# Re-ordering the first tiles of a retention layer with a gated feed-forward: a decay table and v scaled on GpSimd, narrow ups in one bank, half downs with attention steps placed by hand

## The chip, the cores and the metric

The kernel runs on one core of a Trainium2 chip. The metric is the device time of one execution in microseconds; lower is better. Before the change it was 242.91 us (median of 3 runs, 242.81 to 243.11). The span that a profile shows is 1.7 us shorter than the time of the same run. All ratios below are the mean time of one kernel's fast runs over that of the kernel before in the same rounds on the same chip, so they are not quite the ratio of the medians quoted.

## The reference

A retention layer runs token by token for 4 batches and 8 heads of 64, over 768 tokens; its output feeds a feed-forward layer with a sigmoid gate (3072 tokens, 512 wide, 1536 hidden).

```python
def _attn_ref(q, k, v):                       # q, k, v: (4, 8, 768, 64)
    gamma = 1.0 - 2.0 ** (-5.0 - np.arange(H))
    for t in range(S):
        state = gamma * state + outer(k[:, :, t], v[:, :, t])
        y[:, :, t] = scale * (q[:, :, t] @ state)

def _moe_ref(x, w_gate, w_val, w_out):        # x: (3072, 512)
    gate = 1.0 / (1.0 + np.exp(-(x @ w_gate)))
    return (gate * (x @ w_val)) @ w_out
```

## The kernel before

The sequence is cut into 24 chunks of 128 tokens (6 per batch). Within a chunk the recurrence becomes masked matrix products ("scores", "intra"), between chunks a state is carried ("state", "inter"). Decay enters through two tables: `tabv` scales v before use, `taby` scales y on its way out of PSUM. Four chunks make one tile of 512 tokens; a tile needs 12 "ups" (8 matmuls each, gate and value) and 4 "downs" (12 matmuls each). Attention of the next tile is woven between the ups and downs of this one. The order of the program text is the order on every engine: nothing is rescheduled.

Words used below: PE is TensorE, which does the matmuls; in lines of the profile DVE is VectorE, ACT is ScalarE, POOL is GpSimd, and L with a number is a line of that run's kernel. PSUM is the memory that matmuls write, in banks; an eviction copies a result out of it. The granted clock is the share of its full clock that PE was given. Of the tiles, qkT holds the turned q and k of a chunk, sA and sB its scores, vs its scaled v, z its state, y its result and xT that result scaled for the feed-forward; gs is the sigmoid of a gate, hT the product of gate and value, hT(0,0) that of tile 0's first up, and ob a down's result on its way out.

```python
    def load_chunk(g):                # k and q cast to bf16 on the way, v as float32;
        load_kq(g)                    # all issued by GpSimd, as are the weights
        load_v(g, nc.gpsimd)

    def make_taby(cols):              # decay table of y, on ScalarE
        for p in range(NP):
            nc.scalar.activation(taby[:, p, cols], toky[:, cols], AX.Exp, scale=lgp[:, p:p + 1], bias=lsc)

    def transposes(g):                # k, q of a chunk, turned on PE, evicted by ScalarE
        ...
        nc.scalar.activation(qkT[g], tp, AX.Copy)

    def scale_v(g, eng):
        eng.tensor_tensor(vs[g], vf[g], tabv[:, g % NCH, :].unsqueeze(2).to_broadcast([C, H, D]), op=ALU.mult)

    def y_out(g):                     # VectorE
        nc.vector.tensor_tensor(xT[g // 4][:, :, col:col + C], y[g], taby[:, :, c * C:(c + 1) * C], op=ALU.mult)

    def step_t(g):
        if g < XBAR:                  # XBAR = 12: later chunks are transposed by DMA
            transposes(g)
        scale_v(g, nc.vector if g < 8 else nc.gpsimd)

    def step_y(g, nxt=None):
        inter(g)
        if nxt is not None:
            scores(nxt)
        state(g); intra(g); state_out(g)
        if nxt is not None:
            masks(nxt)                # VectorE
        y_out(g)

    def up(t, n1, lo=0, hi=512):      # pf is a ring of three PSUM banks, tag "ff"
        ps = []
        for w in (wg, wv):
            u = pf.tile([128, 512], F32, tag="ff", name="ff")
            ...                       # 4 matmuls
            ps.append(u)
        nc.scalar.activation(gs[:, lo:hi], ps[0][:, lo:hi], AX.Sigmoid)
        nc.vector.tensor_tensor(hT[t][:, n1, lo:hi], gs[:, lo:hi], ps[1][:, lo:hi], op=ALU.mult)

    def keep_on(n):                   # matmuls of no use, meant to keep PE's clock up; they take a bank of the ring too
        u = pf.tile([128, 512], F32, tag="ff", name="ff")
        for _ in range(n):
            nc.tensor.matmul(u[:, :128], ident, ident, start=True, stop=True)

    ...
    scale_v(2, nc.vector)             # the start, chunk after chunk (cut)
    y_out(1)
    ...
    make_taby(slice(512, 768))
    nc.scalar.preload_act_table(AX.Sigmoid)
    intra(2)
    y_out(2)
    scale_v(3, nc.vector)
    keep_on(8)
    up(0, 0, 0, 384)
    transposes(3)
    up(0, 1, 0, 384)
    scores(3)
    ...
    for t in range(NT):
        groups = [lambda n1=n1: up(t, n1) for n1 in range(0 if t else 4, NFF)]
        groups += [lambda sm=sm: down(t, sm) for sm in range(4)]
        steps = attention(t + 1) if t + 1 < NT else []      # nine steps
        ...
        for i, group in enumerate(groups):
            group()
            upto = -(-len(steps) * (i + 1 - first) // (len(groups) - first))
            ...                       # steps spread evenly behind the groups
```

## Time and profile before

| | |
|---|---|
| time | 242.91 us |
| PE busy | 228.8 us (95% of the span) |
| ScalarE, VectorE, GpSimd busy | 95.0, 101.4, 91.5 us |
| PE idle, 0 to 28.65 us | 5.3 us, and 9.0 us of keep-warm matmuls |
| PE idle, 40.7 to 62.2 us | 3.1 us |
| PE idle, 62.2 to 206.1 us | 0.0 us |

The table is read from the bottom: the last row says that the steady tiles have nothing to give, so a gain must come from the first 62 us. A busy PE there is not a useful PE, as the keep-warm matmuls count too. The lines of the profile that carry this stand in the prediction.

### The profile page before, as it was taken

The numbers are of one execution on the slowest core, as the hardware profiler recorded it, in microseconds if no ns is written. First come the engines' busy times: TensorE is split into PE (matmuls) and PEld (weight loads), VectorE is DVE, ScalarE is ACT, GpSimd is POOL, SyncE is SP. The second block draws the span as 40 slices with busy tenths as digits, with TensorE's granted clock in tenths as the row PEclk, the third lists the DMA queues.
The fourth block names the chain that finished last, engine by engine and source line by source line (L and its number), as shares of the span: only waits on it lengthen the run. The fifth ranks groups of instructions, "written<-read, shape, count | busy, mean of one in ns | idle before, by whom it ended". The sixth has DMA issues, their size and how long they took to land.

```text
span 241.1 us, 4300 instructions
## 1 busy us (share of the span) xinstructions
PE 228.8 (95%) x1720; PEld 118.0 (49%) x1720; DVE 101.4 (42%) x168; ACT 95.0 (39%) x179; POOL 91.5 (38%) x111
## 2 busy tenths in 40 slices
PE   7689998998899999999999999999999999999993
PEld 6565644554445554444554445444445554444441
DVE  2565534474256623256632255642256641243300
ACT  7778434343544432334333324232233431333221
POOL 8986674887899446883101101111000000000000
PEclk9999999999999999999999999999999999999999
DMA  8999999999999999999932383002200012100022
GB/s 144 178 200 197 195 208 200 186 196 228 233 179 119 117 153 187 196 160 157 151 51 87 109 91 67 0 16 83 79 3 0 0 46 83 47 3 0 0 87 87
DMA packets 77267, 27.27 MB, mean 113 GB/s; under 512 B 65024, under 2 KB 72704, under 8 KB 77248
## 3 DMA queue, kind: packets, MB, share of 16 engines
q0 software_dynamic: 57616, 16.78, 72.9%
q1 hardware_dynamic: 18592, 9.97, 20.2%
q10 hardware_dynamic: 1040, 0.26, 0.5%
q8 instruction: 13, 0.21, 0.4%
q14 instruction: 6, 0.05, 0.1%
HBM read 28.31 MB, written 6.29 MB: 144 GB/s over the span
## 4 chain that ended last, share of the span: by engine, by line
PE 90%; ACT 7%; issue 1%; DVE 0%; POOL 0%; POOLq 0%; ACTq 0%
PE ff L242 51%; PE ff L252 26%; PE sA L160 3%; ACT qkT L140 3%; PE y L196 2%; ACT taby L123 2%; PE z L182 2%; PE y L172 2%; PE tp L138 2%; PE ff L262 2%; ACT zbd L190 1%; ACT L315 1%; ACT ob L255 0%; ACT gs L246 0%; DVE xT L204 0%
## 5 line engine op out<-in xcount | busy, mean ns | idle before, releaser
L247 DVE TENSOR_TENSOR hT<-gs,ff 128x512 bf16<-128x512 f32 (+2 forms) x76 | 50.0, 659 | 80.3 <-PE ff L242 76.8
L242 PE MATMUL ff<-xT,wg 128*128 128x512 bf16 (+2 forms) x304 | 74.7, 368 | 1.2 <-DVE xT L204 1.1
L242 PE MATMUL ff<-xT,wv 128*128 128x512 bf16 (+2 forms) x304 | 74.6, 368 | 0.0
L246 ACT ACTIVATE gs<-ff 128x512 f32<-128x512 f32 (+2 forms) x76 | 43.7, 574 | 69.3 <-PE ff L242 69.3
L252 PE MATMUL ff<-wo,hT 128*128 128x512 bf16 x288 | 65.0, 379 | 0.0
L242 PEld LDWEIGHTS <-wv 128*128 128x128 bf16 x304 | 29.3, 98 | 33.2
L242 PEld LDWEIGHTS <-wg 128*128 128x128 bf16 x304 | 27.9, 98 | 31.3 <-issue 1.4
L252 PEld LDWEIGHTS <-hT 128*128 128x128 bf16 x288 | 27.3, 98 | 32.1
L150 POOL TENSOR_TENSOR vs<-vf,tabv 128x512 bf16<-128x512 f32 x16 | 16.5, 1046 | 51.2 <-PE y L196 46.3
L255 ACT COPY ob<-ff 128x512 f32<-128x512 f32 x24 | 14.1, 586 | 55.0 <-PE ff L252 50.7
L62 POOL DMA_DIRECT2D vf<-in_v_dram x23 | 20.7, 901 | 12.7 <-DMA kn<-in_k_dram 8.3
L204 DVE TENSOR_TENSOR xT<-y,taby 128x512 bf16<-128x512 f32 x24 | 16.4, 683 | 20.6 <-PE y L196 20.6
L165 DVE TENSOR_TENSOR stA<-sA,causal 128x512 bf16<-128x512 f32 x24 | 16.5, 687 | 19.9 <-PE sB L160 19.9
L67 POOL DMA_DIRECT2D kn<-in_k_dram x23 | 20.8, 905 | 5.7 <-DMA qn<-in_q_dram 1.7
L68 POOL DMA_DIRECT2D qn<-in_q_dram x23 | 20.4, 888 | 3.1 <-DMA wo<-in_moe_w_out_dram 1.7
L190 ACT CAST zbd<-z 64x256 bf16<-64x256 f32 x40 | 14.7, 367 | 12.2 <-PE z L182 11.9
L166 DVE TENSOR_TENSOR stB<-sB,causal 128x512 bf16<-128x512 f32 x24 | 16.3, 680 | 0.0
L140 ACT ACTIVATE qkT<-tp 128x1024 bf16<-128x1024 bf16 x12 | 12.3, 1024 | 4.9 <-PE tp L138 4.8
L262 PE MATMUL ff<-ident 128*128 128x128 bf16 x104 | 9.0, 252 | 1.6 <-POOL ident masks.py:199 1.6
L160 PE MATMUL sA<-qkT 64*128 64x128 bf16 x48 | 4.7, 219 | 5.5 <-ACT qkT L140 5.4
L196 PE MATMUL y<-stA,vs 128*64 128x128 bf16 x96 | 9.9, 222 | 0.0
L196 PE MATMUL y<-stB,vs 128*64 128x128 bf16 x96 | 9.5, 221 | 0.0
(40 smaller groups left out, 107.7 us busy)
## 6 DMA issues: line engine op xcount, KB each, us to landing
out_dram<-ob SPq DMA_DIRECT2D x24, 256.0 KB, 2.0
vf<-in_v_dram POOLq DMA_DIRECT2D x23, 256.0 KB, 8.9
kn<-in_k_dram POOLq DMA_DIRECT2D x23, 128.0 KB, 8.8
qn<-in_q_dram POOLq DMA_DIRECT2D x23, 128.0 KB, 9.1
wg<-in_moe_w_gate_dram POOLq DMA_DIRECT2D x6, 256.0 KB, 8.7
wv<-in_moe_w_val_dram POOLq DMA_DIRECT2D x6, 256.0 KB, 9.1
wo<-in_moe_w_out_dram POOLq DMA_DIRECT2D x4, 384.0 KB, 10.7
qf<-in_q_dram ACTq DMA_DIRECT2D x1, 256.0 KB, 4.5
```

The source lines that it names most:

```text
L62: eng.dma_start(out=vf[g], in_=src(v, g))
L67: nc.gpsimd.dma_start(out=kn[g], in_=src(k, g))
L68: nc.gpsimd.dma_start(out=qn[g], in_=src(q, g))
L140: nc.scalar.activation(qkT[g], tp, AX.Copy)
L150: eng.tensor_tensor(vs[g], vf[g], tabv[:, g % NCH, :].unsqueeze(2).to_broadcast([C, H, D]), op=ALU.mult)
L165: nc.vector.tensor_tensor(stA[g], sc[g][0], causal4, op=ALU.mult)
L190: nc.scalar.copy(zbd[g % 2][half, :, half], zps[b][half])
L196: nc.tensor.matmul(y[g][i * D:(i + 1) * D, p, :], vs[g][:, 2 * p + i, :], st[:, p, :], start=(first and p == 0), stop=True, skip_group_che ...
L242: nc.tensor.matmul(u[:, lo:hi], w[:, kk, n1 * 128:(n1 + 1) * 128], xT[t][:, kk, lo:hi], start=(kk == 0), stop=(kk == KT - 1))
L246: nc.scalar.activation(gs[:, lo:hi], ps[0][:, lo:hi], AX.Sigmoid)
L247: nc.vector.tensor_tensor(hT[t][:, n1, lo:hi], gs[:, lo:hi], ps[1][:, lo:hi], op=ALU.mult)
L252: nc.tensor.matmul(o, hT[t][:, n1, sm * 128:(sm + 1) * 128], wo[:, n1, :], start=(n1 == 0), stop=(n1 == NFF - 1))
```

## The change

Its intent: start the feed-forward earlier and leave no wait in the first tile. On ScalarE, the Exp table is loaded at once and half of `taby` is no longer made there; GpSimd multiplies the first half by a constant per head instead. GpSimd also scales v of chunks 0 and 1. The last 128 columns of the first four ups share a bank each for gate and value. Downs are cut in halves, and the attention steps of tile 0's loop stand at places chosen by hand. At the start of tile 1, the first two ups are split so that chunk 7's last step can come between them. The order of the steps of chunks 0 to 2 and the keep-warm matmuls among them changed too; that part of the diff is cut. The core of the diff:

```diff
-    nc.scalar.dma_start(out=qf, in_=src(q, 0))
+    nc.sync.dma_start(out=qf, in_=src(q, 0))
+    nc.scalar.preload_act_table(AX.Exp)
 ...
+    def extend_taby():
+        nc.gpsimd.tensor_tensor(taby[:, :, 384:768], taby[:, :, 0:384],
+                                gup.unsqueeze(2).to_broadcast([128, NP, 384]), op=ALU.mult)
 ...
+    scale_v(0, nc.gpsimd)
     load_gate_val(0)
+    scale_v(1, nc.gpsimd)
     load_chunk(3)
+    load_gate_val(1)
+    load_gate_val(2)
+    make_taby(slice(0, 256))
 ...
+    make_taby(slice(256, 384))
+    extend_taby()
 ...
-    make_taby(slice(512, 768))
-    nc.scalar.preload_act_table(AX.Sigmoid)
     intra(2)
     y_out(2)
     scale_v(3, nc.vector)
     keep_on(8)
     up(0, 0, 0, 384)
+    up(0, 1, 0, 384)
     transposes(3)
-    up(0, 1, 0, 384)
+    keep_on(16)
     scores(3)
 ...
-    for n1 in range(4):
-        up(0, n1, 384, 512)
+    up_columns(0, range(4), 384, 512)      # four ups' last columns side by side in one bank
 ...
+        groups, steps, place = ups(t) + downs(t), [], []      # downs(t): two halves each
+        if t == 0:
+            groups = groups[4:]
+            steps = [step_t(4), step_s(4), step_y(4), step_t(5), step_s(5),
+                     step_t(6), step_y(5, 6), step_t(7), step_y(6, 7)]      # lambdas left out
+            place = [4, 5, 7, 9, 10, 11, 12, 13, 14]
+        elif t + 1 < NT:
+            steps = attention(t + 1)
+            place = [0, 1, 3, 5, 7, 8, 10, 13, 17]
+        if t == 1:
+            groups[:2] = [up(1, 0, 0, 384), step_y(7), up(1, 1, 0, 384), up_columns(1, range(2), 384, 512)]
+            place = [p + 2 for p in place]
```

More of the change, by code (lines that the diff above doesn't have):

```diff
@@ L97 @@
     make_identity(nc, ident)
-    toky = const.tile([128, S], I32, name="toky")
-    nc.gpsimd.iota(toky, pattern=[[1, S]], base=0, channel_multiplier=0)
+    toky = const.tile([128, 384], I32, name="toky")
+    nc.gpsimd.iota(toky, pattern=[[1, 384]], base=0, channel_multiplier=0)
     load_chunk(1)
@@ L115 @@
         nc.vector.memset(lgp[D:128, p:p + 1], lg[2 * p + 1])
+    gup = const.tile([128, NP], F32, name="gup")
+    for h in range(H):
+        nc.vector.memset(gup[h % 2 * D:(h % 2 + 1) * D, h // 2:h // 2 + 1], math.exp(384 * lg[h]))
     zbd = [const.tile([128, NP, C], BF16, name=f"zbd{i}") for i in range(2)]
@@ L247, in up, with up_columns, down @@
         nc.vector.tensor_tensor(hT[t][:, n1, lo:hi], gs[:, lo:hi], ps[1][:, lo:hi], op=ALU.mult)
-    def down(t, sm):
-        o = pf.tile([128, 512], F32, tag="ff", name="ff")
-        for n1 in range(NFF):
+    def up_columns(t, n1s, lo, hi):
+        n = hi - lo
+        ps = []
+        for w in (wg, wv):
+            u = pf.tile([128, 512], F32, tag="ff", name="ff")
+            for i, n1 in enumerate(n1s):
+                for kk in range(KT):
+                    nc.tensor.matmul(u[:, i * n:(i + 1) * n], w[:, kk, n1 * 128:(n1 + 1) * 128], xT[t][:, kk, lo:hi],
+                                     start=(kk == 0), stop=(kk == KT - 1))
+            ps.append(u[:, :len(n1s) * n])
+        gs = ffn.tile([128, 512], F32, tag="gs", name="gs")
+        g = gs[:, :len(n1s) * n]
+        nc.scalar.activation(g, ps[0], AX.Sigmoid)
+        nc.vector.tensor_tensor(hT[t][:, n1s[0]:n1s[-1] + 1, lo:hi], g.rearrange("p (i n) -> p i n", n=n),
+                                ps[1].rearrange("p (i n) -> p i n", n=n), op=ALU.mult)
+    po = {}
+    def down(t, sm, part):
+        if part == 0:
+            po[0] = pf.tile([128, 512], F32, tag="ff", name="ff")
+        o = po[0]
+        half = NFF // 2
+        for n1 in range(part * half, (part + 1) * half):
             nc.tensor.matmul(o, hT[t][:, n1, sm * 128:(sm + 1) * 128], wo[:, n1, :],
                              start=(n1 == 0), stop=(n1 == NFF - 1))
+        if part == 0:
+            return
         ob = ffn.tile([128, D_MODEL], F32, tag="ob", name="ob")
@@ L262, in keep_on @@
             nc.tensor.matmul(u[:, :128], ident, ident, start=True, stop=True)
+    scale_v(0, nc.gpsimd)
     load_gate_val(0)
+    scale_v(1, nc.gpsimd)
     load_chunk(3)
-    for s in range(1, NFF // 2):
+    load_gate_val(1)
+    load_gate_val(2)
+    make_taby(slice(0, 256))
+    kn[0] = ld.tile([C, H, D], BF16, tag="kn", name="kn")
+    qn[0] = ld.tile([C, H, D], BF16, tag="qn", name="qn")
+    nc.vector.tensor_copy(kn[0], kf)
+    nc.scalar.copy(qn[0], qf)
+    keep_on(36)
+    transposes(0)
+    make_taby(slice(256, 384))
+    extend_taby()
+    for s in range(3, NFF // 2):
         load_gate_val(s)
@@ L273 @@
         load_chunk(g)
-    kn[0] = ld.tile([C, H, D], BF16, tag="kn", name="kn")
-    qn[0] = ld.tile([C, H, D], BF16, tag="qn", name="qn")
-    make_taby(slice(0, 256))
-    nc.vector.tensor_copy(kn[0], kf)
-    nc.scalar.copy(qn[0], qf)
-    keep_on(36)
-    transposes(0)
     keep_on(8)
-    scale_v(0, nc.vector)
     scores(0)
+    masks(0)
+    keep_on(8)
+    transposes(1)
+    inter(0)
     state(0)
     state_out(0)
-    masks(0)
-    keep_on(8)
-    make_taby(slice(256, 384))
-    transposes(1)
-    scale_v(1, nc.vector)
-    inter(0)
     intra(0)
     y_out(0)
-    keep_on(10)
+    keep_on(8)
     scores(1)
+    masks(1)
+    keep_on(4)
+    inter(1)
     state(1)
     state_out(1)
-    masks(1)
-    inter(1)
-    keep_on(10)
-    make_taby(slice(384, 512))
     transposes(2)
+    nc.scalar.preload_act_table(AX.Sigmoid)
     intra(1)
+    y_out(1)
     scale_v(2, nc.vector)
-    y_out(1)
     keep_on(12)
     scores(2)
+    masks(2)
+    inter(2)
     state(2)
     state_out(2)
-    masks(2)
-    inter(2)
-    keep_on(12)
-    make_taby(slice(512, 768))
-    nc.scalar.preload_act_table(AX.Sigmoid)
+    keep_on(10)
     intra(2)
@@ L331, with ups, downs @@
     up(0, 3, 0, 384)
-    for n1 in range(4):
-        up(0, n1, 384, 512)
-    for t in range(NT):
-        groups = [lambda n1=n1: up(t, n1) for n1 in range(0 if t else 4, NFF)]
-        groups += [lambda sm=sm: down(t, sm) for sm in range(4)]
-        steps = attention(t + 1) if t + 1 < NT else []
+    up_columns(0, range(4), 384, 512)
+    def ups(t):
+        return [lambda n1=n1: up(t, n1) for n1 in range(NFF)]
+    def downs(t):
+        return [lambda sm=sm, i=i: down(t, sm, i) for sm in range(4) for i in range(2)]
+    for t in range(NT):
+        groups, steps, place = ups(t) + downs(t), [], []
+        if t == 0:
+            groups = groups[4:]
+            steps = [lambda: step_t(4), lambda: step_s(4), lambda: step_y(4), lambda: step_t(5), lambda: step_s(5),
+                     lambda: step_t(6), lambda: step_y(5, 6), lambda: step_t(7), lambda: step_y(6, 7)]
+            place = [4, 5, 7, 9, 10, 11, 12, 13, 14]
[3 more added lines that the diff above has]
+        if t == 1:
+            groups[:2] = [lambda: up(1, 0, 0, 384), lambda: step_y(7), lambda: up(1, 1, 0, 384),
+                          lambda: up_columns(1, range(2), 384, 512)]
+            place = [p + 2 for p in place]
         if t + 2 < NT:
@@ L342 @@
                 load_chunk(g)
-        first = 0 if t else 6
-        done = 0
         for i, group in enumerate(groups):
-            if i == len(groups) - 5:
+            if i == len(groups) - 9:
                 for g in range(4 * t + 8, 4 * t + 12):
@@ L350 @@
             group()
-            upto = -(-len(steps) * (i + 1 - first) // (len(groups) - first))
-            while done < min(upto, len(steps)):
-                steps[done]()
-                done += 1
+            for p, step in zip(place, steps):
+                if p == i:
+                    step()
 _INS = ['q', 'k', 'v', 'moe_w_gate', 'moe_w_val', 'moe_w_out']
```

## The prediction

> **What bounds the kernel now.** I read the page first, then the chain that ended last, the waits of the PE, the stretches by window, and the timeline of the first 65 us with the landings of its loads.
>
> ```profile
> PE   7689998998899999999999999999999999999993
> ACT  7778434343544432334333324232233431333221
> DMA  8999999999999999999932383002200012100022
> ```
>
> Each digit is 6 us. PE is full from about 28 us to the end, apart from a dip between 40 and 62; in the windows view 62.15 to 206.10 holds 143.95 us of PE in 143.95. So only the first 62 us can give anything. The feed-forward is fixed: a 512-wide up (8 matmuls) takes 1.73 us and a down (12) 2.59 in the chain, so six tiles need 6 x (12 x 1.73 + 4 x 2.59) = 186.7 us whatever the order. DMA is near full from the start: a second possible bound there.
>
> The chain (start, length, what):
>
> ```profile
> 13.26 1.65 ACT taby L123 x4
> 14.93 1.03 ACT qkT L140
> ...
> 17.51 2.07 ACT taby L123 x4
> 19.60 1.28 ACT L315
> 20.89 0.49 ACT gs L246
> 21.39 0.92 ACT qkT L140
> 22.35 0.23 PE sA L160
> ...
> 41.38 1.03 ACT qkT L140
> ...
> 56.03 1.03 ACT qkT L140
> ...
> 61.41 0.70 DVE xT L204
> ```
>
> Until 22 us ScalarE is the bound: the decay tables (taby) stand in its queue ahead of the transposes' evictions (qkT), then the sigmoid table load, and chunk 3's scores start only at 22.35. Later PE waits three times where an attention step follows the work it needs too closely.
>
> ```profile
> PE sA L160 <- ACT qkT L140: 5.4, 5, 1.3
> PE ff L242 <- DVE xT L204: 1.1, 2, 0.8
> ```
>
> Of these the timeline puts 1.12 at 42.46, 1.18 at 57.11 and 0.79 at 62.15: 3.09 us between 40 and 62, which agrees with the windows view (18.34 busy in 21.42). The timeline of the first ups:
>
> ```profile
> 11.59 0.96 POOL L62 DMA_DIRECT2D vf<-in_v_dram  x1
> 15.96 0.75 POOL L81 DMA_DIRECT2D wg<-in_moe_w_gate_dram  x1 [0.43 <-DMA wv<-in_moe_w_val_dram]
> 18.88 0.68 DVE L150 TENSOR_TENSOR vs<-vf,tabv 128x512 bf16<-128x512 f32 x1
> 19.02 0.81 PE L242 MATMUL ff<-xT,wg 128*128 128x384 bf16 x4 [0.30 <-DVE xT L204]
> 26.32 0.39 PE L242 MATMUL ff<-xT,wg 128*128 128x128 bf16 x4
> 28.65 1.02 PE L242 MATMUL ff<-xT,wg 128*128 128x512 bf16 x4
> ```
>
> The first line is the load of chunk 3's v, which the tile view says takes 7.0 us to land: at 18.6, just before VectorE scales it (18.88). First up at 19.02, last columns from 26.32, first full-width up at 28.65. I count from these marks.
>
> **What the Trainium skill says.** (1) "SBUF — State Buffer", Who interferes with whom: a VectorE instruction with two SBUF inputs and a GpSimd instruction that reads SBUF exclude each other for the whole instruction; the later one blocks. scale_v is such an instruction, masks and evictions (one PSUM input) are not. Before, GpSimd computes nothing with it in the first 60 us, so the trace cannot show this. (2) "GPSIMD Engine Reference", Elementwise — side-by-side cycle accounting: about 2.6 cycles an element for two inputs, GpSimd some 2x slower. The trace agrees in kind:
>
> ```profile
> L150 POOL TENSOR_TENSOR vs<-vf,tabv 128x512 bf16<-128x512 f32 x16 | 16.5, 1046 | 51.2 <-PE y L196 46.3 <-issue 4.9
> L150 DVE TENSOR_TENSOR vs<-vf,tabv 128x512 bf16<-128x512 f32 x8 | 5.5, 684 | 1.7 <-DMA vf<-in_v_dram 1.7
> ```
>
> (3) "ScalarE: Activation LUTs", Table-load gate, puts a load at about 2.7 us with its drain; here the row reads 1.28, so I use that. (4) "TensorE: Matmul & The Clock Gate", Back-to-back issue gap and its phases: 55.6 ns a 128-wide matmul, 215.7 a 512-wide. The trace: 0.22 us for four and 1.73 for eight. It agrees.
>
> **The change part by part.**
>
> ScalarE. taby for columns 384 to 767 leaves it: 1.65 + 2.07 = 3.72 us of the chain above; the third 128 columns move ahead of the second qkT. The Exp table load starts about 0.5 earlier. Walking the new order with these durations: qkT0 ends 7.3, taby 9.0, qkT1 10.0, z of chunk 0 after v on GpSimd (about 9.1), zbd0 10.8, scores(1) 10.2, z of chunk 1 waits for GpSimd's second v (11.6), zbd1 12.7, qkT2 13.7, table load 15.0, masks(2) 15.6, y_out(2) 16.7. The first up then starts at about 16.8, 2.3 us earlier.
>
> GpSimd. It is also the issuer of loads. iota loses 0.38 (half of 0.77). Two v scalings add 2 x 1.05. The taby extension, 1536 columns, is an estimate of 3 x 1.05 = 3.1 us. After walking: v0 at 8.0 to 9.05, wg0 issued 9.0 (before 8.38), v1 10.5 to 11.55, chunk 3's v issued at 13.25 (before 11.59), extension from about 17.1 to 20.2, then the fourth weight slab at 20.2 (before 15.96). The delays mostly eat queueing: loads took 5.0 us while the queue was short and 7 to 10 later. I put chunk 3's v at 19.0 (before 18.6). Slab 1 lands about 21.5 and is wanted after 22; later weights keep 2 us or more.
>
> VectorE. In its order chunk 3's scaling stands ahead of the first hT. That was harmless (hT waited for the sigmoid until 21.42); with the first up ending at 18.1 it is a new wait. hT(0,0) comes after the load at 19.0 plus 0.3 plus 0.69, and, if the skill's exclusion holds, only after the extension (20.2). The 16 keep-warm matmuls take the PSUM buffer that hT(0,0) frees (ring of three, counted through the allocations), and scores(3) stand behind them. So scores(3) start at 19.3 + 0.69 + 0.55 + 1.0 = about 21.6 without exclusion, 20.3 + 2.25 = about 22.6 with it; before 22.35. Of the 2.3 us won, -0.2 to 0.8 remain at this place.
>
> Columns. The 32 narrow matmuls took 28.65 - 26.32 = 2.33 with 0.33 of waiting for a bank; in one bank 32 x 0.055 = 1.76. Gain 0.6. First full-width up: 27.3 without, 28.3 with exclusion. Gain 1.35 or 0.35.
>
> Attention between half downs in tile 0. With a step between half downs (1.3 us each) or ups, qkT (1.03) has time. I find small waits left: 0.15 for qkT5 and qkT7 (the ob copy stands ahead of them on ScalarE), 0.35 for y_out(6) before tile 1's first up (masks(7) precede it), 0.25 for qkT8 after the two short columns. 3.09 - 0.75 = 2.3 us gained.
>
> Steady tiles. The hand places 0,1,3,5,7,8,10,13,17 over 20 groups are what the old formula gave over 16, with a down counted as two halves: no change. The tail too: 0.
>
> Sum: 1.35 + 2.3 = 3.65, or 0.35 + 2.3 = 2.65. 242.91 less these is 239.3 or 240.3. As some later waits (a short load, a bank) can also vanish with the narrow ups, I take **239.5**.
>
> **Rivals.** (a) Full gain: v of chunk 3 lands by 18 us or the block at hT is not there. Then scores(3) wait only for qkT3 (about 20.95), up 4 starts at 26.7, 1.95 + 2.3 + some = 4.5: 238.4. For it: DMA is the only thing I had to estimate. Against: its digits are 9 there and GpSimd issues later. (b) Loads become the bound: the GpSimd work delays weights and chunks 4 to 7 by its full 5.2 - 0.4 us. wo's last part landed at 41.8 and chunk 5's q at 43.7; the new order wants them at about 44 and 45.5. Then the gain of the middle is lost: 241.5 to 242.5. Against: at most eight loads are in flight and issues already wait for landings (the 0.43 above), so idle issue time absorbs most. (c) Exclusion as the skill has it: 240.3, within my range.
>
> **Range and chances.** My two main cases are 239.3 and 240.3, (a) makes 238.4 and (b) 242. The range that should hold it 8 in 10: 237.9 to 241.0. Faster by over 2% needs 238.05: beyond (a), 0.15. Slower: 0.01. Within 2%: 0.84.
>
> **What would show it.** First up near 16.8; scores(3) at 21.5 to 22.7, with keep-warm matmuls waiting on VectorE's hT just before; chunk 3's scaling either 0.69 long near 19.3 or lengthened or begun when the extension ends; first full-width up at 27.3 to 28.3; the middle's waits under 1 us; 62 us to the end unchanged in length. It is wrong if PE waits on weights or chunk loads, if scores(3) start before 21, or if the steady tiles change.

## The result, and the profile after

The changed kernel took 240.39 us in its first four runs (239.64, 239.81, 240.97, 240.97), a ratio of 0.9893 (0.9856 to 0.9930): inside the range of 237.9 to 241.0, and within 2%. The two levels of its time were not foreseen. The profiled run took 239.81 us, a span of 238.1 against 241.1 before.

The chain that ended last, of the changed kernel (start, length, what), from the first up to the first full-width up:

```profile
16.98 2.77 PE ff L250 x16
...
20.58 0.55 DVE hT L255
21.18 1.05 PE ff L293 x16
22.23 0.16 PE sA L168
...
26.29 1.79 PE ff L264 x32
28.08 0.21 PE ff L250
```

The first up is 2.0 us earlier (16.98 against 19.02), but chunk 3's scores are only 0.2 us earlier (22.16 in the timeline against 22.35). Between them the chain runs through VectorE's hT and the 16 keep-warm matmuls. The timeline says why hT was late (start, length, engine, line, operation; in brackets the idle time before it and what ended it):

```profile
17.27 2.83 POOL L130 TENSOR_TENSOR taby<-taby,gup 128x1536 f32<-128x1536 f32 x1
...
18.47 2.18 DVE L158 TENSOR_TENSOR vs<-vf,tabv 128x512 bf16<-128x512 f32 x1 [1.55 <-DMA vf<-in_v_dram]
...
20.58 1.00 DVE L255 TENSOR_TENSOR hT<-gs,ff 128x384 bf16<-128x384 f32 x2
...
21.18 1.05 PE L293 MATMUL ff<-ident 128*128 128x128 bf16 x16 [0.99 <-DVE hT L255]
```

VectorE's scaling of chunk 3's v took 2.18 us in place of the 0.68 that it took before, and it ended at 20.65, 0.55 after the table extension on GpSimd (20.10). The narrow columns took 1.79 us in place of 2.33, so that the first full-width up starts at 27.91 in the timeline: 0.74 earlier than before.

From there on PE hardly waits. The list of PE's waits in the changed kernel, cut to those after 24 us:

```profile
PE ff L281 <- issue: 0.2, 1, 0.2
...
PE sA L168 <- ACT qkT L148: 0.3, 1, 0.3
PE z L190 <- POOL vs L158: 0.2, 1, 0.2
```

The 3.09 us of the middle are gone but for 0.3. The last line is new: the state of chunk 8 waits for its v, which GpSimd scales. A mark in the timeline sums this up (before, changed kernel, and, for a later experiment, the kernel before with the new places alone):

```profile
66.47 1.04 PE L242 MATMUL ff<-xT,wg 128*128 128x512 bf16 x4
...
63.23 1.04 PE L250 MATMUL ff<-xT,wg 128*128 128x512 bf16 x3
...
64.07 1.04 PE L242 MATMUL ff<-xT,wg 128*128 128x512 bf16 x4
```

The full-width up that follows chunk 8's scores started at 66.47 before and starts at 63.23 now, 3.24 us earlier: 0.74 from the start and 2.50 from the middle. The span is 3.0 us shorter, so some 0.25 us are given back after that mark, most of them at that new line.

### The profile page after: what moved, and what is told of

The parts are those of the page before. It is cut to its first block, busy times and chain, and to the rows that moved or that the text cites. A ratio compares the mean times of both kernels' runs of the same rounds, so it can differ in the third digit from the quotient of the medians.

```text
span 238.1 us, 4313 instructions
## 1 busy us (share of the span) xinstructions
PE 227.8 (96%) x1716; PEld 118.9 (50%) x1742; DVE 102.0 (43%) x172; ACT 90.8 (38%) x169; POOL 95.9 (40%) x114
## 4 chain that ended last, share of the span: by engine, by line
PE 88%; POOL 6%; issue 2%; ACT 2%; DVE 1%; ACTq 0%; POOLq 0%; DVEq 0%
PE ff L250 49%; PE ff L281 26%; PE sA L168 3%; PE y L204 2%; PE z L190 2%; PE y L180 2%; PE tp L146 2%; POOL vs L158 1%; POOL kn L67 1%; POOL vf L62 1%; POOL qn L68 1%; ACT qkT L148 1%; PE ff L264 1%; ACT ob L286 1%; PE ff L293 1%
## 5 line engine op out<-in xcount | busy, mean ns | idle before, releaser
L255 DVE TENSOR_TENSOR hT<-gs,ff 128x512 bf16<-128x512 f32 (+1 forms) x72 | 48.6, 676 | 75.5 <-PE ff L250 73.9
L250 PE MATMUL ff<-xT,wg 128*128 128x512 bf16 (+1 forms) x276 | 71.5, 375 | 0.9 <-DVE xT L212 0.3
L250 PE MATMUL ff<-xT,wv 128*128 128x512 bf16 (+1 forms) x282 | 71.9, 375 | 0.4
L254 ACT ACTIVATE gs<-ff 128x512 f32<-128x512 f32 (+1 forms) x72 | 42.3, 588 | 68.8 <-PE ff L250 68.3
L250 PEld LDWEIGHTS <-wv 128*128 128x128 bf16 x288 | 28.2, 98 | 32.7
L250 PEld LDWEIGHTS <-wg 128*128 128x128 bf16 x288 | 26.7, 98 | 30.2 <-issue 0.8
L158 POOL TENSOR_TENSOR vs<-vf,tabv 128x512 bf16<-128x512 f32 x18 | 18.6, 1048 | 47.1 <-PE y L204 42.1
L293 PE MATMUL ff<-ident 128*128 128x128 bf16 x110 | 9.5, 251 | 2.6 <-POOL ident masks.py:199 1.6
L293 PEld LDWEIGHTS <-ident 128*128 128x128 bf16 x110 | 8.0, 114 | 3.2 <-POOL ident masks.py:199 1.6
```

The source lines that it names most:

```text
L250: nc.tensor.matmul(u[:, lo:hi], w[:, kk, n1 * 128:(n1 + 1) * 128], xT[t][:, kk, lo:hi], start=(kk == 0), stop=(kk == KT - 1))
```

## The experiments

Twelve experiments ran, in three calls of four; those of one call ran on one chip. Each is told with its edit.

### The changed kernel again

No edit: it is the control, and asks where the two levels come from.

> The changed kernel itself, unaltered, as the control for the other runs of this call and to see the spread (its first runs were 239.6, 239.8, 241.0 and 241.0 us). Expected 240.4, 2.5 us under the kernel before. All theories expect chunk 3's v scaling on VectorE near 2.2 us long, the 16 keep-warm matmuls waiting about 1 us, scores(3) at about 22.2. If the two levels of its time are two places where the loads land, the profile shows another landing of chunk 3's v or another wait; if not, a lower granted clock.

It took 240.04 us (239.67 to 240.87), ratio 0.9889 (0.9876 to 0.9902). The profile fell on the slowest of the five runs (240.87). It shows the same start (chunk 3's scaling 2.27 us, the keep-warm matmuls waiting 1.00), and one thing that differs. The state of chunk 8, in the timelines of the first profile of the changed kernel and of this one:

```profile
71.47 0.32 PE L190 MATMUL z<-vs,kn 128*64 128x64 bf16 x8 [0.15 <-POOL vs L158]
```

```profile
71.45 4.05 POOL L158 TENSOR_TENSOR vs<-vf,tabv 128x512 bf16<-128x512 f32 x4
...
72.56 0.32 PE L190 MATMUL z<-vs,kn 128*64 128x64 bf16 x8 [1.18 <-POOL vs L158]
```

Here GpSimd begins its four scalings (chunks 8 to 11) at 71.45, behind its loads for later chunks, instead of 70.35, and PE waits 1.18 us instead of 0.15. The spans differ by 1.1 us (239.2 and 238.1). So between these two runs the time follows the moment at which GpSimd gets through its loads. The delay can be traced further: the load of v that stands ten instructions ahead of the scalings was issued at 60.30 in the first profile and at 61.63 here, after GpSimd had waited 0.92 us for an earlier load of k to land. The other three runs (240.03 to 240.39) lie between the two levels, so it is a spread and not a switch.

### Chunk 3's scaling behind the first ups

```diff
     y_out(2)
-    scale_v(3, nc.vector)
     keep_on(8)
     up(0, 0, 0, 384)
     up(0, 1, 0, 384)
+    scale_v(3, nc.vector)
     transposes(3)
```

> Only change: chunk 3's v is scaled behind the two first ups in VectorE's order. Theory A (hT stands behind a scaling that GpSimd's table extension blocks): hT(0,0) runs at about 18.3, the keep-warm matmuls wait for nothing, scores(3) start when the eviction of chunk 3's transposes ends, about 21.2 instead of 22.2, and 0.9 us are won there; of it 0.5 to 0.9 reaches the end. Rival B (the load of chunk 3's v is what counts): hT moves but state(3) then waits for v3, scores or z of chunk 3 gain under 0.2 and the time is that of the control. Rival C (the gain is eaten later, where chunk 8's v is scaled on GpSimd at 71.4): scores(3) gain 0.9 but the wait for chunk 8's v grows from 0.15 to about 1 and the time is within 0.2 of the control.

It took 240.30 us (four runs from 240.00 to 240.40, two at 242.55 and 242.54), ratio 0.9921 (0.9887 to 0.9955): not faster than the control. Yet the edit did what theory A said. hT(0,0) ran at 18.57, nothing held the keep-warm matmuls, the scaling (now at 20.34, with the extension over) took 0.69, and scores(3) started at 21.32, 0.84 earlier than in the first profile of the changed kernel. The gain was eaten where rival C put it, in PE's list of waits:

```profile
PE z L190 <- POOL vs L158: 2.4, 2, 2.1
```

PE comes to chunk 8 earlier, GpSimd does not. The runs at 242.5 have more: the windows view (length of the stretch, busy time of PE, PEld, DVE, ACT and POOL, granted clock, DMA share, GB/s) shows a granted clock of 0.50 from 74 to 76 us in the profiled one, after PE had stood idle for 2.06 us.

```profile
74.00:76.00 2.00, 2.00 (x6) 0.76 (x5) 0.00 (x0) 0.60 (x1) 2.00 (x3) 0.50 3.36 113
```

Finer windows put the clock of one half from 73.7 to 77.2 (0.74 granted from 73.5 to 74.0, 0.50 after it, 0.84 from 77.0 to 77.5). In those 3.4 us PE does half its work, so about 1.7 us are lost. This is the profiled run; the other run at 242.5 and the four fast ones have no profile, so how long their idle stretch was is not known. The mean granted clock, which every run lists, agrees: 0.993 and 0.991 in these two, 0.997 to 1.000 in the four. A low mean alone is no proof, though: a run of the kernel with the new places alone has 0.990 and took only some 0.3 us longer than that kernel's others. Theory A holds for the start; rival C fits the time.

### v of chunks 0 and 1 on VectorE

```diff
-    scale_v(0, nc.gpsimd)
     load_gate_val(0)
-    scale_v(1, nc.gpsimd)
 ...
+    scale_v(0, nc.vector)
     keep_on(36)
     transposes(0)
 ...
     masks(0)
+    scale_v(1, nc.vector)
```

> Only change: v of chunks 0 and 1 back on VectorE, chunk 1's ahead of y_out(0); the table extension stays on GpSimd. GpSimd then issues everything 2.1 us earlier and the extension runs from about 15.1 to 18.0, before chunk 3's v lands. Theory A: the scaling of chunk 3's v takes 0.7 instead of 2.2, keep-warm matmuls wait for nothing, scores(3) at about 21.2, time 0.5 to 0.9 under the control. If the intent of the change holds (VectorE is the tight engine there), the first up comes later than 17.0 and the time rises by 0.3 to 1.

It took 239.34 us (238.75 to 239.71), ratio 0.9843 (0.9831 to 0.9856), faster than the control. Two lines of its timeline:

```profile
15.11 2.87 POOL L130 TENSOR_TENSOR taby<-taby,gup 128x1536 f32<-128x1536 f32 x1
...
18.51 0.69 DVE L158 TENSOR_TENSOR vs<-vf,tabv 128x512 bf16<-128x512 f32 x1 [1.60 <-DMA vf<-in_v_dram]
```

The extension is over at 18.0, before chunk 3's v is there, and the scaling takes 0.69. The first up still starts at 16.96 and scores(3) at 21.28. VectorE had room for both scalings, so this part of the change bought nothing, and by pushing the extension onto the scaling of chunk 3 it cost 0.9 us at scores(3). PE waits 0.94 us for chunk 8's v in the profiled run, which hides a part of that in the time.

### A table extension that reads nothing

Its output is wrong, which doesn't matter for the time. The extension becomes two iotas of the same total length into a tile that nobody reads, and y of chunks 3 to 5 is scaled with the tables of chunks 0 to 2.

```diff
-        nc.gpsimd.tensor_tensor(taby[:, :, 384:768], taby[:, :, 0:384], gup..., op=ALU.mult)
+        for i in range(2):
+            nc.gpsimd.iota(junk, pattern=[[1, 1416]], base=i, channel_multiplier=0)
 ...
-        ... taby[:, :, c * C:(c + 1) * C]
+        ... taby[:, :, c % 3 * C:(c % 3 + 1) * C]
```

> Wrong result on purpose: the table extension is replaced by two GpSimd iotas of the same total length (2 x 1416 columns, about 2.8 us) into a tile that nobody reads, and y_out of chunks 3 to 5 takes the tables of chunks 0 to 2. They write SBUF and read none. Theory A in the form of the exclusion between reads: chunk 3's v scaling takes 0.7 us although GpSimd is as busy, hT(0,0) ends near 19.7 and scores(3) at about 21.2. Rival: any busy GpSimd blocks it (or the scaling waits for data still landing): it takes 2 us or more again and scores(3) stay at 22.2.

Its timeline:

```profile
17.27 2.77 POOL L132 IOTA junk<- 128x1416 int32 x2
...
18.49 0.69 DVE L159 TENSOR_TENSOR vs<-vf,tabv 128x512 bf16<-128x512 f32 x1 [1.55 <-DMA vf<-in_v_dram]
```

GpSimd is busy over the same 2.8 us and the data land at the same time, but the scaling takes 0.69 us and scores(3) start at 21.31. So it is neither a busy GpSimd nor data still landing that stretches the scaling. The iotas differ from the extension in two ways, though: they read nothing, and they are another operation. That the reading is what counts is therefore the prediction's form of the exclusion, which fits, and not shown by this run alone. The first profile of the changed kernel fits its other half: GpSimd's scaling of chunk 0, which reads SBUF (8.08 to 9.15), ran beside two masks on VectorE, which have one input in PSUM, and these took 0.69 and 0.68 us. The one time of this run, 242.62 us, carries the same loss as the slow runs with chunk 3's scaling behind the first ups: PE waits 2.1 us for chunk 8's v, and the granted clock is 0.50 from 74 to 76 us (0.96 from 73.5 to 74.0 and 0.63 from 77.0 to 77.5, so one half from about 74.0 to 77.4).

### v of chunks 8 to 11 on VectorE

```diff
-        scale_v(g, nc.vector if g < 8 else nc.gpsimd)
+        scale_v(g, nc.vector if g < 12 else nc.gpsimd)
```

> Only change to the changed kernel: v of chunks 8 to 11 is scaled on VectorE instead of GpSimd, where four scalings stood behind the loads of chunks 4 to 11. Theory (what is won early is partly lost at 71 us, where PE waits 0.15 to 1.2 us for chunk 8's v, and this makes the two levels of the time): the wait is gone, no run is over 240.0, median 239.6 (0.989 to 0.986 of before). Rival (the levels come from something else, such as loads or the clock): runs of 241 remain. Chunk 3's scaling still takes 2.2 us and scores(3) start at 22.2.

It took 239.55 us (239.54, 239.55, 239.55, 239.97), ratio 0.9863 (0.9850 to 0.9877). No run is over 240.0, against six of the nine of the changed kernel, and PE has no wait at chunk 8 in the profile. Together with the two profiles above, whose spans differ by 1.1 us and whose waits by 1.03, this shows that GpSimd's scalings behind its loads made the levels. The start is as in the changed kernel.

### Both edits

Chunk 3's scaling behind the first ups, and v of chunks 8 to 11 on VectorE.

> Chunk 3's scaling behind the two first ups, and v of chunks 8 to 11 on VectorE. Theory: the 0.9 us won at scores(3) (21.3 instead of 22.2) now reach the end, and the granted clock does not fall, as PE has no idle stretch of 2 us at 71: 238.8, that is 0.8 under the run with the second edit alone. Rival (another later wait takes it): within 0.2 of that run, with a new wait in the PE's list.

It took 238.71 us, four runs from 238.69 to 238.72, ratio 0.9824 (0.9811 to 0.9838). That is 0.84 us under the run with the second edit alone on the same chip: what the first edit gains at scores(3) now reaches the end, and the four times agree within 0.03 us.

### A combination

v of chunks 0 and 1 on VectorE as above, v of chunks 8 to 11 too, and two small moves:

```diff
+        if nxt == 7:
+            y_out(g)
         if nxt is not None:
             masks(nxt)
-        y_out(g)
+        if nxt != 7:
+            y_out(g)
 ...
             place = [p + 2 for p in place]
+            place[1] = 4          # scores(8) one group later
```

> Candidate: v of chunks 0, 1 and 8 to 11 on VectorE, y_out(6) ahead of masks(7) on VectorE, scores(8) one group later. Expected: the wait for hT(0,0) gone (0.9), the wait of tile 1's first up for y_out(6) gone (0.3), that of scores(8) for its eviction gone (0.3), that for chunk 8's v gone: 238.2, under both kernels. If VectorE becomes tight, PE waits for stB or hT appear and it stays above 239.

It took 238.21 us (237.78 to 238.75), ratio 0.9807 (0.9794 to 0.9821): 1.9% under the kernel before, and correct; whether that is over 2% is unclear by the interval. It has the lowest median of all, but its interval overlaps that of the kernel with both edits. After 24 us PE's list of waits holds one entry of 0.2 us. Its runs spread over 1 us again, with no scaling of chunk 8 on GpSimd, so there is another source of spread; no run here tells which.

### The placement undone

All of the change except the loop over tiles, which is the old one with whole downs.

> One part undone: whole downs and the old formula for where attention steps go, also in tile 0 and at the start of tile 1; all else as changed. Prediction's step (2.3 us from placement): the three waits come back near 41, 56 and 60 us (1.1, 1.2 and 0.8) and the first full-width up stays at 28.1. As PE is then later at chunk 8, the wait for its v goes: 242.0 (the control less nothing but plus 2.3, less the 0.15 to 1.2 of that wait: 241.1 to 242.2). Rival (the start is what gained): under 240.8.

It took 242.93 us (242.58 to 243.58), ratio 1.0003 (0.9990 to 1.0015): the kernel before, although the first full-width up starts at 27.93. I had expected 241.1 to 242.2. The waits for qkT (1.2 and 1.1) and xT (0.8) are back as expected; what I had left out is in its timeline:

```profile
44.85 0.40 PE L146 MATMUL tp<-ident,qn 128*128 128x128 bf16 x4 [0.59 <-DMA qn<-in_q_dram]
```

With the old places chunk 5 is transposed ahead of the first down, and now it meets a load that has not landed. Two things bring this about. PE comes 0.65 us earlier (the transposes of k start at 43.87 instead of 44.52), and the load of q itself is later: it was issued at 33.33 and landed at 44.8, where before the change it was issued at 32.81 and landed at 43.7. By these marks PE would not have waited with the old landing. So the new start delays the load that eats its gain; the up after chunk 8's scores starts at 66.59, as before (66.47). The new places transpose chunk 5 behind the first down, and PE has no wait for that load.

### The placement alone

The kernel before with the new loop over tiles (half downs, places, split first ups of tile 1) and nothing else.

> The kernel before with the placement part alone: half downs, hand-placed steps in tile 0 and the split first ups of tile 1; the start as before. The prediction's ledger gives 2.3 us: 240.6, and the first full-width up stays at 28.65. As undoing the placement brought the changed kernel back to 242.9, the start seems to be worth nothing without it; if that is symmetric, 240.4 here; if the two parts need each other, over 241.5.

It took 240.38 us (240.26 to 240.63), ratio 0.9899 (0.9885 to 0.9912). The control, the whole change, has 0.9889 (0.9876 to 0.9902). The placement makes most or all of the gain; what the new start adds to it in the time is 0.1% by these means, which come from two chips and whose intervals overlap. In the profile of this kernel the first full-width up is at 28.75, the up after chunk 8's scores at 64.07, 2.40 earlier than before; PE does not wait for chunk 8's v. In the changed kernel that same up starts at 63.23, 0.84 earlier, and the wait for chunk 8's v takes a part of that or all of it. Where this wait is removed (v of chunks 8 to 11 on VectorE, 0.9863), the whole change is 0.36%, or some 0.9 us, under the placement alone: the start is then worth what its mark says, again by two chips.

### Narrow ups one at a time

On the kernel with v of chunks 8 to 11 on VectorE:

```diff
-    up_columns(0, range(4), 384, 512)
+    for n1 in range(4):
+        up(0, n1, 384, 512)
```

> To the changed kernel with v of chunks 8 to 11 on VectorE (239.55 in its own rounds), one part undone: the last 128 columns of the four first ups again one up at a time. Prediction's step: 32 matmuls take 2.3 instead of 1.8 us and the time rises by 0.55 to 240.1. Rival: the bank was not what they waited for, under 0.2.

It took 240.35 us (240.24 to 241.00), ratio 0.9901 (0.9887 to 0.9915), against 0.9863 of its base in another call. In the profiles the first full-width up moves from 27.92 to 28.46 and the up after chunk 8's scores from 63.23 to 63.78: 0.55 both times. The bank was what they waited for, and the size of the step is right. The ratios make it 0.9 us. The spans of the profiled runs differ by 0.6 (238.4 and 237.8); the rest lies outside the span, as this is the one kernel in which time and span differ by 1.9 to 2.0 us in all runs. Why, no run tells.

### The tables on ScalarE again

On the same base, without the extension:

```diff
     make_taby(slice(256, 384))
-    extend_taby()
 ...
     transposes(2)
+    make_taby(slice(384, 768))
     nc.scalar.preload_act_table(AX.Sigmoid)
```

> To the same base: the tables of columns 384 to 767 are made on ScalarE again, ahead of the sigmoid table load, and GpSimd has no extension. If ScalarE must be relieved there (the prediction's first part), gs and the eviction of chunk 3's transposes come later and the time rises by about 1. My theory: ScalarE has just enough room now (2.5 us of tables from 13.9, table load to 17.7, zbd to 18.5, gs0 to 19.0, eviction from 20.2), and chunk 3's scaling on VectorE is no longer blocked (0.7 us): scores(3) at 21.3 and 238.8, 0.75 under the base.

It took 239.15 us (238.85 to 239.60), ratio 0.9848 (0.9834 to 0.9862), against 0.9863 (0.9850 to 0.9877) of the base: not slower. Two lines of its timeline:

```profile
13.95 2.49 ACT L127 ACTIVATE taby<-toky,lsc,lgp 128x384 f32<-128x384 int32 x4
...
18.67 0.69 DVE L158 TENSOR_TENSOR vs<-vf,tabv 128x512 bf16<-128x512 f32 x1 [1.60 <-DMA vf<-in_v_dram]
```

ScalarE makes the tables between two evictions, the first up starts at 17.12, the scaling is not blocked and scores(3) start at 21.45 instead of 22.16. The full-width ups start 0.7 us earlier (27.20). A later wait of 0.6 us (at 98.06) for ScalarE's copy of a down result takes most of that back in the profiled run, the slowest of the four; why it comes there I did not find. On this base, what the change needed was the place of the tables in ScalarE's queue, not that they leave it.

### Keep-warm matmuls in the idle stretch at chunk 8

```diff
             scores(nxt)
+        if g == 8:
+            keep_on(32)
         state(g)
```

This stands on the kernel with chunk 3's scaling behind the first ups, v of chunks 8 to 11 still on GpSimd.

> late_v3 (chunk 3's scaling behind the first ups; 240.0 to 240.4 in four runs, 242.5 in two with a granted clock of 0.993) with 32 keep-warm matmuls between the scores and the state at chunk 8, where PE stood idle for 2.1 us. If the idle stretch is what lowers the clock (0.50 granted at 74 to 76 us), the clock stays at 1.0 and all runs are at 240.0 to 240.5. Rival (the clock falls by chance or by load): runs of 242.5 remain at the same rate.

It took 240.64 us, four runs from 240.62 to 240.69, ratio 0.9908 (0.9895 to 0.9922). No run is at 242.5, the granted clock from 74 to 76 us is 1.00 in the profile, and the mean clock of the four runs is 0.997 to 1.000. It agrees with the idle stretch as the cause. It does not settle it: at two slow runs in six, four fast ones in a row come by chance about once in five, and I have the length of the idle stretch only of profiled runs. What the profiles give: 2.06 and 2.1 us idle, and the clock fell (two of two); 1.2 us or less idle, and it did not.

## Why the prediction was right or wrong

The number and the class were right: 239.5 with 237.9 to 241.0, measured 240.39 and 240.04. Of its two main cases the second, with the exclusion (240.3), has the start that happened; I had blended it with the first. That its number is within 0.1 to 0.3 us of the medians is in part luck: the marks gained 3.24 us, 0.6 more than this case says, and 0.24 (first profile) to 1.3 us (the second) of it were lost at a place that stood in none of my cases. Point by point:

- **The first up.** Predicted 16.8, measured 16.98, so 2.0 us earlier (the "2.3 us" of the prediction is 2.2 by its own marks). Walking the new order of ScalarE, GpSimd and VectorE with the old durations was good to 0.2 us.
- **The wait in its place.** Predicted: chunk 3's scaling blocked until the extension ends, hT(0,0) behind it, the keep-warm matmuls behind the bank of hT(0,0), scores(3) at 22.6. Measured: 22.16, each link in the timeline. The iotas rule out a busy GpSimd and late data, and moving either end (v of chunks 0 and 1, or chunk 3's scaling) removes the wait. The load of chunk 3's v landed at 18.4, not 19.0; had the extension not been there, this term would have been 0.6 too late.
- **The columns.** Predicted 0.6, measured 0.55.
- **The middle.** Predicted 2.3, measured 2.50: the waits left over were somewhat shorter than I thought.
- **Steady tiles "no change".** This is the step that failed. The order of the steps is the same, but I did not ask what an earlier PE meets there. Before the change GpSimd had chunk 8's v ready in time; 3 us earlier it has not, as its scalings stand behind loads whose issue waits for landings (the 0.92 us above). The wait measures 0.15 us in one profile and 1.18 in another, and it is the reason for the two levels. On the mean it costs some 0.6 us, an estimate from the ratios with and without it (0.9889 and 0.9863, two chips).
- **Rival (b), loads as the bound.** I gave it small weight, and in the changed kernel no chunk load holds PE after 24 us. But a mild form of it is the reason why the start is worth nothing without the placement: there chunk 5's q lands 1.1 us later than before the change and holds PE for 0.59 us.
- **The credit.** The prediction gave the start 0.35 to 1.35 us and the placement 2.3. The placement alone gives nearly what the whole change gives (0.9899 and 0.9889, with overlapping intervals); the start's 0.74 us are won at 28 us and for the most part lost again at chunk 8.
- **The rates of the matmuls.** The two figures in the prediction's point (4) agree with the trace, but on the page they stand under "Step-by-step: what each phase is for".

## What to carry to other kernels

An engine that is not the bottleneck can still hold the one that is: before moving elementwise work to GpSimd, look at which VectorE instructions with two SBUF inputs fall into the same stretch, and which loads GpSimd issues behind it. After every gain near the start, follow the earlier engine to the next place where it meets work that did not get earlier, as a load or a queue behind loads; a gain that does not reach the end is seen by comparing marks along the timeline. Where the time has levels, compare the profile of a slow run with that of a fast one before looking for more speed.

## What the Trainium skill lacked or had wrong

- "SBUF — State Buffer", Who interferes with whom, agrees, where the exclusion held up the start: a VectorE product of two SBUF operands (0.69 us alone) ran for 2.18 and 2.27 us beside a GpSimd product that reads SBUF, and 0.69 beside iotas. It does not say how a blocked VectorE instruction looks in a trace: it shows as started (18.47) and long, not as waiting.
- "GPSIMD Engine Reference", Elementwise — side-by-side cycle accounting: about 2x slower than VectorE, measured on an add of 2048 float32 columns; here, for a product, 1046 against 684 ns for 512 columns to bf16, a factor of 1.5, and 2.83 us for 1536 columns to float32, 1.84 ns a column.
- "TensorE: Matmul & The Clock Gate", What's actually happening, puts the fall of the clock after an idle window of about 3.4 us; here gaps of 2.06 and 2.14 us were followed, 1.2 to 1.4 us after their end, by a granted clock of 0.50 for 3.4 us, in both kernels profiled with so long a gap, and gaps of up to 1.2 us at the same place were not. A gap well short of the window can be enough; whether every gap of 2 us is, no run here shows.
- "ScalarE: Activation LUTs", Table-load gate: about 2.7 us for a load with its drain; here no drain shows. The row in the trace reads 1.28 us, which is what the page gives for the load alone, and the work behind it started 1.3 us after its start (the work ahead of it ended at 17.51 + 2.07 = 19.58, load at 19.60, gs at 20.89).
